# The order in which one-pass matmuls read their moving columns, in an attention and mixer kernel on Trainium2

## The chip, the cores and the metric

The kernel runs on one core of a Trainium2 chip. The metric is the device time of one execution in microseconds (us); lower is better. Runs of the kernel before are given by their median.

## What is computed

Chunked softmax attention on 8 batches, 8 heads, 576 tokens and 64 columns per head, in chunks of 64 tokens, then a mixer on the result: a token layer across the 576 tokens and a channel layer across the 512 columns, each with a hidden layer and a ReLU.

```python
def _attn_ref(q, k, v):          # (8, 8, 576, 64); chunks of 64 tokens
    scores = np.matmul(q_c, k_c.transpose(0, 1, 2, 4, 3)) / np.sqrt(64)
    attn = np.exp(scores - scores.max(-1, keepdims=True))
    attn = attn / (attn.sum(-1, keepdims=True) + 1e-09)
    return np.matmul(attn, v_c)
def _moe_ref(x, w_tok1, w_tok2, w_ch1, w_ch2):   # x (8, 576, 512)
    h = np.maximum(x.transpose(0, 2, 1) @ w_tok1, 0.0) @ w_tok2   # 576 -> 256 -> 576
    u = x + h.transpose(0, 2, 1)
    return u + np.maximum(u @ w_ch1, 0.0) @ w_ch2                 # 512 -> 1536 -> 512
```

## The kernel before, in words

All data is float32, and the result has to be accurate beyond what one pass of TensorE in the type `F32R` gives. So most products are made of three matmuls in F32R: each operand is split into a high part and a low part, and high x high, low x high and high x low are added in one PSUM bank (the table `THREE`). Each of these matmuls takes one pass over its moving operand; they are called one-pass below. Plain float32 matmuls go through the engine in two recorded passes; they are left for the attention and the first batch.

- **Attention** (`attn_s`, `attn_both`, `attn_v`): 64 x 64 pieces in plain float32, in bursts between the mixer's matmuls.
- **Token layer, first product** (`tok1_part`, L565): 512 moving columns; `tok1_end` (L582, L583) takes the ReLU out of the bank and splits it, ScalarE the high part, VectorE the low part.
- **Token layer, second product** (`block_mix`, L636): the moving operand is a piece of the weights as wide as the batch border leaves it, 64 to 512 columns; VectorE adds x to the bank (L642). The first batch has its own form in plain float32 (`tok2`, L609).
- **Channel layer, direct** (`ch1` L664, `ch2` L706): batch 0 in halves of 288 tokens, then two blocks of 512 tokens. `ch1` leaves its bank to ScalarE (L675, or L672) and VectorE (L676); `ch2` adds up over 12 rounds in four banks that VectorE reads at the end (L714).
- **Channel layer, in pairs** (`pair`, `pair_end`): three pairs of blocks, two of them 512 and the last 480 tokens wide. A 2 x 2 product is made with seven multiplications in place of eight: `product` (L1030) makes each in one of two banks (`ps_c1`), `snap` (L1117, ScalarE) and `plus` (L1122, VectorE) read it, and `ch2_half` (L1099) adds into four banks (`ps_acc`) that `finish` reads (L1110).

The order of the work is partly written out by hand (bursts and steps in tables), partly fixed from a simulated schedule when the kernel is built; SyncE issues all transfers. Every moving operand of a one-pass matmul is read column after column, and every bank that it fills is read column after column. A VectorE or ScalarE read of a bank covers 288 to 512 columns in one instruction.

Of the kernel before, what the change touches and what calls it, by code (L numbers as in the profile page):

```python
# [8 lines left out]
F32 = mybir.dt.float32  # L9
# [4 lines left out]
F32R = mybir.dt.float32r  # L14
# [51 lines left out]
SUMS = ((3, 5, 7), (11, 13, 14), (18, 20, 22), (25, 27, 28), (32, 34, 35), (38, 40, 41))  # L66

AHEAD = 3

# [14 lines left out]
JOBS = [(9, "ready")]  # L86
JOBS += [(s, "part", j, k) for j, ss in enumerate(STARTS) for k, s in enumerate(ss)]
JOBS += [(s, "split", i) for i, s in enumerate(SPLIT_AT)]


@with_exitstack
def attention_mixer_kernel(ctx, tc, qk_in, vo_in, v_in, w1_in, w2_in, wc1_in, wc2_in, out):
# [187 lines left out]
    def block_x(k):  # L280

        if k not in xts:
            xts[k] = pool.tile([P, N // BK, NDT, BK], F32, tag="xt", name="xt")
        return xts[k]
# [267 lines left out]
    def tok1_part(b, m, n, ps):  # L552
        mt = mix_tiles(b)
        if b % 2:
            mt = mt[-1:] + mt[:-1]
        t, rows, j = mt[n]
        w = weights["t1", j][:, :, m * P:(m + 1) * P]
        if j == 4 and b:
            st = tiles[t]["stack"][b % 2]
            terms = ((w[:, 0], st), (half_low[b % 2][:, m * P:(m + 1) * P], st))  # L560
        else:
            xs = (tiles[t]["xh"], tiles[t]["xl"])
            terms = [(w[rows, wi], xs[xi][rows]) for wi, xi in THREE]
        for q, (lhsT, rhs) in enumerate(terms):
            nc.tensor.matmul(  # L565
                ps, lhsT=lhsT, rhs=rhs,
                start=(n == 0 and q == 0), stop=(n == len(mt) - 1 and q == len(terms) - 1),
            )

# [9 lines left out]
    def tok1_end(ps):  # L579
        rh = pool.tile([P, DM], F32R, tag="gr", name="rh", bufs=12)  # L580
        rl = pool.tile([P, DM], F32R, tag="gr", name="rl", bufs=12)
        nc.scalar.activation(out=rh, in_=ps, func=AF.Relu)  # L582
        nc.vector.scalar_tensor_tensor(  # L583
            out=rl, in0=ps, scalar=0.0, in1=rh.bitcast(F32), op0=ALU.max, op1=ALU.subtract
        )
        return rh, rl

# [36 lines left out]
    def block_mix(k, rs, m, ps):  # L624

        cols = slice(m * P, (m + 1) * P)
        base, width = BLOCKS[k]
        at = 0
        while at < width:
            b, lo = divmod(base + at, S)  # L630
            n = min(S - lo, width - at)
            terms = [
                (rs[b + 1][t][ri], weights["t2", t][:, wi, lo:lo + n]) for t in range(NT1) for wi, ri in THREE
            ]
            for q, (lhsT, rhs) in enumerate(terms):
                nc.tensor.matmul(  # L636
                    ps[:, at:at + n], lhsT=lhsT[:, cols], rhs=rhs,
                    start=(q == 0), stop=(q == len(terms) - 1),
                )
            at += n  # L640
        u = pool.tile([P, N], F32, tag="u", name="u", bufs=8)[:, :width]
        nc.vector.tensor_tensor(  # L642
            out=u.rearrange("p (i c) -> p i c", c=BK),
            in0=ps[:, :width].rearrange("p (i c) -> p i c", c=BK),
            in1=block_x(k)[:, :width // BK, m], op=ALU.add,
        )
        return u

# [9 lines left out]
    def ch1(u, f, kept=False, width=HALF):  # L658
        while ("c1", f) not in weights:
            convert(1)  # L660
        ps = ps_c1.tile([P, 512], F32, tag="c1", name="ps_c1")
        for k in range(NDT):
            for q, (wi, ui) in enumerate(THREE):
                nc.tensor.matmul(  # L664
                    ps[:, :width], lhsT=weights["c1", f][:, wi, k // 2, k % 2 * P:(k % 2 + 1) * P], rhs=u[ui][k],
                    start=(k == 0 and q == 0), stop=(k == NDT - 1 and q == 2),
                )
        if kept:
            if "g1" not in tiles:
                tiles["g1"] = pool.tile([P, NFC, HALF], F32, tag="g1", name="g1", bufs=1)  # L670
            g = tiles["g1"][:, f]
            nc.scalar.activation(out=g, in_=ps[:, :HALF], func=AF.Relu)  # L672
            return g
        gh, gl = g_parts(width)
        nc.scalar.activation(out=gh, in_=ps[:, :width], func=AF.Relu)  # L675
        nc.vector.scalar_tensor_tensor(  # L676
            out=gl, in0=ps[:, :width], scalar=0.0, in1=gh.bitcast(F32), op0=ALU.max, op1=ALU.subtract
        )
        return gh, gl

# [9 lines left out]
    def ch2(at, width, u, f, g, accs):  # L690

        while ("c2", f) not in weights:
            convert(1)
        whole = at + width == B * S
        if f == 0:
            accs[:] = [ps_acc.tile([P, 512], F32, tag="acc", name="acc")[:, :width] for _ in range(NDT)]
        if f == NFC - 2 and whole:
            for e in range(NDT):
                o = pool.tile([P, N], F32, tag="o", name="o", bufs=8)[:, :width]
                nc.gpsimd.tensor_tensor(  # L700
                    out=o, in0=u[0][e].bitcast(F32), in1=u[1][e].bitcast(F32), op=ALU.add
                )
                accs.append(o)
        for e in range(NDT):
            for q, (wi, gi) in enumerate(THREE):
                nc.tensor.matmul(  # L706
                    accs[e], lhsT=weights["c2", f][:, wi, e * P:(e + 1) * P], rhs=g[gi],
                    start=(f == 0 and q == 0), stop=(f == NFC - 1 and q == 2),
                )
            if f < NFC - 1:  # L710
                continue
            o = accs[NDT + e] if whole else pool.tile([P, N], F32, tag="o", name="o", bufs=8)[:, :width]
            base = o if whole else u[0][e].bitcast(F32)
            nc.vector.tensor_tensor(out=o, in0=accs[e], in1=base, op=ALU.add)  # L714
            if not whole:
                on_pool = at < S or REST_ON_POOL[(at - S) // N][e]
                (nc.gpsimd if on_pool else nc.vector).tensor_tensor(
                    out=o, in0=o, in1=u[1][e].bitcast(F32), op=ALU.add
                )
            nc.sync.dma_start(out=out[e, :, at:at + width], in_=o)  # L720
# [302 lines left out]
    def product(i, u, width):  # L1023

        load_product(i + RING - 1)
        ps = ps_c1.tile([P, 512], F32, tag="c1", name="ps_p")[:, :width]
        w = ring[i]
        for j in range(2):
            for q, (wi, ui) in enumerate(THREE):
                nc.tensor.matmul(  # L1030
                    ps, lhsT=w[:, wi, j * P:(j + 1) * P].bitcast(F32R), rhs=u[ui][j],
                    start=j == 0 and q == 0, stop=j == 1 and q == 2,
                )
        return ps
# [60 lines left out]
    def ch2_half(f, g, accs, es, start, stop):  # L1095

        for e in es:
            for q, (wi, gi) in enumerate(THREE):
                nc.tensor.matmul(  # L1099
                    accs[e], lhsT=weights["c2", f][:, wi, e * P:(e + 1) * P], rhs=g[gi],  # L1100
                    start=start and q == 0, stop=stop and q == 2,
                )

# [3 lines left out]
    def finish(e, acc, at, width, base, rest=None, on_pool=1):  # L1107

        o = pool.tile([P, N], F32, tag="o", name="o", bufs=8)[:, :width]
        nc.vector.tensor_tensor(out=o, in0=acc, in1=base, op=ALU.add)  # L1110
        if rest is not None:
            (nc.gpsimd if on_pool else nc.vector).tensor_tensor(out=o, in0=o, in1=rest, op=ALU.add)
        nc.sync.dma_start(out=out[e, :, at:at + width], in_=o)

    def snap(ps, width):
        s = pool.tile([P, N], F32, tag="snap", name="snap", bufs=2)[:, :width]
        nc.scalar.copy(out=s, in_=ps)  # L1117
        return s

    def plus(a, b, width, tag, engine=None):  # L1120
        c = pool.tile([P, N], F32, tag=tag, name=tag, bufs={"g2": NFC, "sum": 3}.get(tag, 1))[:, :width]
        (engine or nc.vector).tensor_tensor(out=c, in0=a, in1=b, op=ALU.add)  # L1122
        return c

    def split_sum(c, width, relu=True):
# [7 lines left out]
    def pair(n, rs):  # L1133
# [7 lines left out]
        for p in range(NFC // 2):  # L1141
# [5 lines left out]

            low, high = range(2), range(2, NDT)
            p1 = snap(product(i, own[0], width), width)
            c11 = plus(product(i + 1, own[1], width), p1, width, "c11")  # L1150
            step(0)
            if pend is not None:
                ch2_half(2 * p - 1, pend, accs, low, False, False)
            step(1)
            u2 = plus(product(i + 2, own[2], width), p1, width, "sum")
            g1 = split_sum(c11, width)
            p5 = snap(product(i + 3, own[3], width), width)
            step(2)
            if pend is not None:
                ch2_half(2 * p - 1, pend, accs, high, False, False)  # L1160
            step(3)
            u3 = plus(product(i + 4, own[4], width), u2, width, "sum")
            u4 = plus(p5, u2, width, "sum", nc.gpsimd)
            later[2 * p + 1] = plus(p5, u3, width, "g2", nc.gpsimd)
            c21 = plus(product(i + 5, own[5], width), u3, width, "c21")
            step(4)
            ch2_half(2 * p, g1, accs, low, p == 0, False)
            step(5)
            pend = split_sum(c21, width)
            later[2 * p] = plus(product(i + 6, own[6], width), u4, width, "g2")  # L1170
            step(6)
            ch2_half(2 * p, g1, accs, high, p == 0, False)
            step(7)
# [155 lines left out]
```

## Time and profile before

| | us |
|---|---|
| median of 3 runs (lowest, highest) | 769.34 (768.42, 770.45) |
| span of the profiled execution, first to last instruction | 765.0 |
| TensorE busy (weight loads beside it) | 748.2 (629.2) |
| VectorE, ScalarE, GpSimd busy | 436.0, 276.4, 190.4 |

The profiled execution is shown by its span alone; what lies around the span is not in the page. The median of the runs is 4.3 us above that span. TensorE is busy for 98% of the span, but the ends of matmuls are modelled, and the records overlap: a matmul of 512 columns is shown with some 390 ns, while the next one starts after some 227 ns. What one matmul takes of the engine is therefore read as the distance from its start to the next start.

### The profile page before, as it was taken

How to read it: one execution, taken by the hardware profiler on the slowest of the kernel's cores; microseconds unless marked ns; L12 is line 12 of the kernel's file. 1: busy time of each engine (PE TensorE's matmuls, PEld its weight loads, DVE VectorE, ACT ScalarE, POOL GpSimd, SP SyncE). 2: the span in 40 equal slices, each digit the busy share in tenths (PEclk: the TensorE clock that was granted, in tenths of full speed). 3: DMA queues.
4: the chain of work that ended last, by engine and by line, in shares of the span. 5: the costliest groups of instructions: out<-in, count | busy, mean ns of one | idle time of the engine just before them, and what ended most of it. 6: DMA issues, size and time to landing. Idle time of an engine off the chain costs nothing.

```text
span 765.0 us, 14620 instructions
## 1 busy us (share of the span) xinstructions
PE 748.2 (98%) x5730; PEld 629.2 (82%) x5730; DVE 436.0 (57%) x735; ACT 276.4 (36%) x505; POOL 190.4 (25%) x161
## 2 busy tenths in 40 slices
PE   6899999999999999999999999999999999999998
PEld 4489998888888887888888888988888888888886
DVE  5799956554447356687567643875343348323361
ACT  6899933242333334342232232432212233111220
POOL 0000002434336544031121162141221503211120
PEclk8999999999999999999999999999999999999999
DMA  9956346687844676817878863056445421634011
GB/s 356 406 190 219 109 146 203 219 251 255 290 157 159 226 231 200 278 66 262 273 239 290 276 228 82 2 186 196 142 138 165 162 60 59 217 113 133 29 53 51
DMA packets 93268, 139.94 MB, mean 183 GB/s; under 512 B 10832, under 2 KB 44880, under 8 KB 93200
## 3 DMA queue, kind: packets, MB, share of 16 engines
q1 hardware_dynamic: 93200, 139.02, 55.1%
q8 instruction: 45, 0.74, 0.4%
q14 instruction: 23, 0.19, 0.1%
HBM read 98.34 MB, written 39.71 MB: 180 GB/s over the span
## 4 chain that ended last, share of the span: by engine, by line
PE 87%; ACT 5%; DMA 3%; DVE 3%; issue 1%; SPq 1%; ACTq 0%
PE acc L1099 25%; PE ps_p L1030 22%; PE acc L706 11%; PE ps_c L664 10%; PE ps_t L636 7%; PE ps_t L565 6%; PE ps_sv L356 2%; DMA raw_t<-in_w 2%; PE ps_sv L368 2%; ACT low L190 1%; ACT wtop L189 1%; PE sum L574 1%; DMA far<-blocks 1%; ACT low L199 1%; DVE wtop L209 1%
## 5 line engine op out<-in xcount | busy, mean ns | idle before, releaser
L1099 PE MATMUL acc<-gh,kept_c 128*128 128x512 f32 (+1 forms) x576 | 176.2, 387 | 0.0
L1030 PE MATMUL ps_p<-bh,ring 128*128 128x512 f32 (+1 forms) x504 | 154.3, 387 | 0.0
L1099 PEld LDWEIGHTS acc<-gh,kept_c 128*128 128x128 f32 x576 | 107.4, 188 | 20.6
L1099 PE MATMUL acc<-gl,kept_c 128*128 128x512 f32 (+1 forms) x288 | 111.1, 386 | 0.0
L1030 PEld LDWEIGHTS ps_p<-bh,ring 128*128 128x128 f32 x504 | 94.0, 188 | 18.2
L1030 PE MATMUL ps_p<-bl,ring 128*128 128x512 f32 (+1 forms) x252 | 97.2, 386 | 0.0
L706 PE MATMUL acc<-gh,kept_c 128*128 128x288 f32 (+1 forms) x384 | 93.8, 346 | 1.0 <-ACT gh L675 0.9
L468 POOL TENSOR_TENSOR xl<-x,xh 128x512 fp32r<-128x512 f32 x28 | 38.1, 1372 | 168.0 <-ACT xh L467 148.6
L706 PEld LDWEIGHTS acc<-gh,kept_c 128*128 128x128 f32 x384 | 63.4, 188 | 9.5 <-ACT gh L675 1.6
L1122 POOL TENSOR_TENSOR sum<-snap,sum 128x512 f32<-128x512 f32 (+1 forms) x18 | 23.3, 1292 | 179.5 <-ACT snap L1117 155.2
L1099 PEld LDWEIGHTS acc<-gl,kept_c 128*128 128x128 f32 x288 | 54.0, 188 | 10.4
L664 PE MATMUL ps_c<-uh,kept_c 128*128 128x512 f32 x192 | 59.8, 393 | 0.0
L706 PE MATMUL acc<-gl,kept_c 128*128 128x288 f32 (+1 forms) x192 | 58.3, 343 | 0.0
L1030 PEld LDWEIGHTS ps_p<-bl,ring 128*128 128x128 f32 x252 | 47.3, 188 | 9.1
L1127 ACT ACTIVATE gh<-c 128x512 fp32r<-128x512 f32 (+1 forms) x36 | 22.4, 623 | 81.8 <-DVE c L1122 81.8
L336 ACT ACTIVATE pr<-pr 128x512 f32<-128x512 f32 x36 | 22.7, 630 | 79.9 <-DVE pr L332 79.9
L1117 ACT COPY snap<-ps_p 128x512 f32<-128x512 f32 (+1 forms) x36 | 20.8, 579 | 84.5 <-PE ps_p L1030 77.0
L676 DVE SCALAR_TENSOR_TENSOR gl<-ps_c,gh 128x512 fp32r<-128x512 f32 (+1 forms) x36 | 21.8, 605 | 45.1 <-ACT gh L675 45.0
L1128 DVE SCALAR_TENSOR_TENSOR gl<-g,gh 128x512 fp32r<-128x512 f32 (+1 forms) x36 | 30.7, 874 | 29.0 <-ACT gh L1127 29.0
L664 PE MATMUL ps_c<-both,kept_c 128*128 128x288 f32 x288 | 43.7, 299 | 0.1
L664 PEld LDWEIGHTS ps_c<-uh,kept_c 128*128 128x128 f32 x192 | 35.5, 188 | 7.5
L664 PEld LDWEIGHTS ps_c<-both,kept_c 128*128 128x128 f32 x288 | 39.5, 188 | 1.1 <-DVE gl L676 0.4
(134 smaller groups left out, 1260.2 us busy)
## 6 DMA issues: line engine op xcount, KB each, us to landing
ring<-w SPq DMA_DIRECT2D x126, 256.0 KB, 3.5
qk<-in_qk SPq DMA_DIRECT2D x36, 512.0 KB, 4.9
far<-blocks SPq DMA_DIRECT2D x63, 256.0 KB, 2.7
raw_c<-in_wc SPq DMA_DIRECT2D x24, 512.0 KB, 9.4
pf<-far SPq DMA_DIRECT2D x124, 64.0 KB, 2.5
v<-in_v SPq DMA_DIRECT2D x27, 256.0 KB, 4.3
xt<-far SPq DMA_DIRECT2D x96, 64.0 KB, 2.1
w<-sparts SPq DMA_DIRECT2D x24, 256.0 KB, 2.8
```

The source lines that it names most:

```text
L336: nc.scalar.activation(out=pr, in_=pr, func=AF.Exp, scale=1.0 / float(D) ** 0.5)
L468: nc.gpsimd.tensor_tensor(out=xl, in0=t["own"], in1=xh.bitcast(F32), op=ALU.subtract)
L565: nc.tensor.matmul(ps, lhsT=lhsT, rhs=rhs, start=(n == 0 and q == 0), stop=(n == len(mt) - 1 and q == len(terms) - 1),)
L636: nc.tensor.matmul(ps[:, at:at + n], lhsT=lhsT[:, cols], rhs=rhs, start=(q == 0), stop=(q == len(terms) - 1),)
L664: nc.tensor.matmul(ps[:, :width], lhsT=weights["c1", f][:, wi, k // 2, k % 2 * P:(k % 2 + 1) * P], rhs=u[ui][k], start=(k == 0 and q == 0) ...
L676: nc.vector.scalar_tensor_tensor(out=gl, in0=ps[:, :width], scalar=0.0, in1=gh.bitcast(F32), op0=ALU.max, op1=ALU.subtract)
L706: nc.tensor.matmul(accs[e], lhsT=weights["c2", f][:, wi, e * P:(e + 1) * P], rhs=g[gi], start=(f == 0 and q == 0), stop=(f == NFC - 1 and ...
L1030: nc.tensor.matmul(ps, lhsT=w[:, wi, j * P:(j + 1) * P].bitcast(F32R), rhs=u[ui][j], start=j == 0 and q == 0, stop=j == 1 and q == 2,)
L1099: nc.tensor.matmul(accs[e], lhsT=weights["c2", f][:, wi, e * P:(e + 1) * P], rhs=g[gi], start=start and q == 0, stop=stop and q == 2,)
L1122: (engine or nc.vector).tensor_tensor(out=c, in0=a, in1=b, op=ALU.add)
L1127: nc.scalar.activation(out=gh, in_=c, func=AF.Relu)
L1128: nc.vector.scalar_tensor_tensor(out=gl, in0=c, scalar=0.0, in1=gh.bitcast(F32), op0=ALU.max, op1=ALU.subtract)
```

## The change

Every one-pass matmul of the mixer reads its moving operand in another order of columns. Where the operand is whole (`tok1_part`, `ch1`, `ch2`, `product`, `ch2_half`), it reads column 0, then the first column of the second half, then column 1, and so on. In `block_mix` it takes each group of eight columns in the order 0, 4, 1, 5, 2, 6, 3, 7. The PSUM bank is written column after column as before, so its columns now stand in that order, and every instruction of ScalarE or VectorE that reads the bank reads every second column, first the even ones and then the odd ones (in fours in `block_mix`), which puts its output back in natural order. The same instructions run on every engine's queue in the same order as before; only access patterns differ. The plain float32 matmuls (attention, L574, L609) are as before.

```diff
+RUN = 4
+def in_turn_of_two(ap):
+    return ap.rearrange("p (a b) -> p b a", a=2)
+def in_order(ps):
+    return ps.rearrange("p (b a) -> p a b", a=2)
+def halved(ap):
+    return ap.rearrange("p (a b) -> p a b", a=2)
...
             nc.tensor.matmul(
-                ps, lhsT=lhsT, rhs=rhs,
+                ps, lhsT=lhsT, rhs=in_turn_of_two(rhs),
...
-        nc.scalar.activation(out=rh, in_=ps, func=AF.Relu)
+        ps = in_order(ps)
+        nc.scalar.activation(out=halved(rh), in_=ps, func=AF.Relu)
         nc.vector.scalar_tensor_tensor(
-            out=rl, in0=ps, scalar=0.0, in1=rh.bitcast(F32), op0=ALU.max, op1=ALU.subtract
+            out=halved(rl), in0=ps, scalar=0.0, in1=halved(rh.bitcast(F32)), op0=ALU.max, op1=ALU.subtract
...
-                    ps[:, at:at + n], lhsT=lhsT[:, cols], rhs=rhs,
+                    ps[:, at:at + n], lhsT=lhsT[:, cols],
+                    rhs=rhs.rearrange("p (c a b) -> p c b a", a=2, b=RUN),
...
         nc.vector.tensor_tensor(
-            out=u.rearrange("p (i c) -> p i c", c=BK),
-            in0=ps[:, :width].rearrange("p (i c) -> p i c", c=BK),
-            in1=block_x(k)[:, :width // BK, m], op=ALU.add,
+            out=u.rearrange("p (i c a b) -> p i c a b", c=BK // (2 * RUN), a=2, b=RUN),
+            in0=ps[:, :width].rearrange("p (i c b a) -> p i c a b", c=BK // (2 * RUN), b=RUN, a=2),
+            in1=block_x(k)[:, :width // BK, m].rearrange("p i (c a b) -> p i c a b", a=2, b=RUN), op=ALU.add,
...
-                    ps, lhsT=w[:, wi, j * P:(j + 1) * P].bitcast(F32R), rhs=u[ui][j],
+                    ps, lhsT=w[:, wi, j * P:(j + 1) * P].bitcast(F32R),
+                    rhs=in_turn_of_two(u[ui][j]),
...
-        nc.scalar.copy(out=s, in_=ps)
+        nc.scalar.copy(out=halved(s), in_=in_order(ps))
...
+        if inside:
+            nc.vector.tensor_tensor(out=halved(c), in0=in_order(a), in1=halved(b), op=ALU.add)
+        else:
+            engine.tensor_tensor(out=c, in0=a, in1=b, op=ALU.add)
```

The places left out repeat these forms: `ch1`, `ch2` and `ch2_half` read `in_turn_of_two(...)`, their banks are read with `in_order` into `halved` outputs, and the calls of `plus` that read a bank say `inside=True`.

## Rows read from the trace of the kernel before

**Rows 1.** The page: span, TensorE's busy time, its granted clock in 40 slices.
```profile
span 765.0 us, 14620 instructions
...
PE 748.2 (98%) x5730; PEld 629.2 (82%) x5730; DVE 436.0 (57%) x735; ACT 276.4 (36%) x505; POOL 190.4 (25%) x161
...
PEclk8999999999999999999999999999999999999999
```
**Rows 2.** The page: the chain that ended last, shares of the span by engine.
```profile
PE 87%; ACT 5%; DMA 3%; DVE 3%; issue 1%; SPq 1%; ACTq 0%
```
**Rows 3.** Waits of TensorE: waiting line, releaser, us in total, times, longest us.
```profile
PE acc L706 <- ACT gh L675: 0.9, 2, 0.7
```
**Rows 4.** Groups of TensorE by shape: count, then busy us and mean ns (modelled ends).
```profile
L1099 PE MATMUL acc<-gh,kept_c 128*128 128x512 f32 x384 | 119.1, 391 | 0.0
...
L1030 PE MATMUL ps_p<-bh,ring 128*128 128x512 f32 x336 | 104.3, 392 | 0.0
...
L1099 PE MATMUL acc<-gh,kept_c 128*128 128x480 f32 x192 | 57.1, 378 | 0.0
...
L664 PE MATMUL ps_c<-both,kept_c 128*128 128x288 f32 x288 | 43.7, 299 | 0.1
```
**Rows 5.** Timeline of TensorE, 512 columns, six matmuls from first to last row: start us, us, count.
```profile
400.12 0.62 PE L1099 MATMUL acc<-gh,kept_c 128*128 128x512 f32 x2
...
401.48 0.62 PE L1030 MATMUL ps_p<-bh,ring 128*128 128x512 f32 x2
```
**Rows 6.** The same, 480 columns: twelve matmuls from first to last row.
```profile
700.01 0.59 PE L1030 MATMUL ps_p<-bh,ring 128*128 128x480 f32 x2
...
702.62 0.59 PE L1030 MATMUL ps_p<-bh,ring 128*128 128x480 f32 x2
```
**Rows 7.** The same, 288 columns, batch 0: 27 matmuls from first to last row.
```profile
99.78 2.14 PE L664 MATMUL ps_c<-both,kept_c 128*128 128x288 f32 x15
...
103.33 0.95 PE L664 MATMUL ps_c<-both,kept_c 128*128 128x288 f32 x6
```
**Rows 8.** The same, 256 columns in `block_mix`: eighteen matmuls between these two.
```profile
476.60 0.40 PE L636 MATMUL ps_t<-again,rh 128*128 128x256 f32 x2
...
478.76 0.46 PE L636 MATMUL ps_t<-again,rh 128*128 128x320 f32 x2
```
**Rows 9.** The same, 192 columns.
```profile
481.39 0.27 PE L636 MATMUL ps_t<-again,rl 128*128 128x192 f32 x1
481.50 0.39 PE L636 MATMUL ps_t<-again,rh 128*128 128x192 f32 x2
```
**Rows 10.** The same, plain float32, 288 columns: second to fourth pass of one bank.
```profile
40.60 0.41 PE L609 MATMUL ps_t<-wtt,r 128*128 128x288 f32 x1
...
40.84 0.41 PE L609 MATMUL ps_t<-wtt,r 128*128 128x288 f32 x1
...
41.08 0.41 PE L609 MATMUL ps_t<-wtt,r 128*128 128x288 f32 x1
```
**Rows 11.** Groups of ScalarE and VectorE by shape: count, busy us, mean ns, idle.
```profile
L467 ACT CAST xh<-x 128x512 fp32r<-128x512 f32 x28 | 16.4, 616 | 3.3 <-DVE x L447 3.3
...
L189 ACT ACTIVATE wtop<-raw_c 128x512 f32<-128x512 f32 x24 | 16.4, 682 | 0.7 <-DMA raw_c<-in_wc 0.7
...
L675 ACT ACTIVATE gh<-ps_c 128x288 fp32r<-128x288 f32 x12 | 4.9, 408 | 1.4 <-PE ps_c L664 1.4
...
L1122 DVE TENSOR_TENSOR sum<-ps_p,snap 128x512 f32<-128x512 f32 x12 | 8.2, 687 | 3.5 <-PE ps_p L1030 3.4
...
L676 DVE SCALAR_TENSOR_TENSOR gl<-ps_c,gh 128x288 fp32r<-128x288 f32 x12 | 5.4, 452 | 6.6 <-ACT gh L675 6.5
```
**Rows 12.** Busy us by stretch: PE, weight loads, DVE, ACT, POOL, clock, DMA share, GB/s.
```profile
45.00:160.00 115.00, 112.42 (x1063) 103.59 (x1060) 86.93 (x171) 73.76 (x146) 21.32 (x21) 1.00 0.53 172
...
395.00:505.00 110.00, 110.00 (x763) 92.51 (x762) 68.82 (x102) 36.53 (x66) 33.78 (x24) 1.00 0.56 178
```

More of the change, by code (lines that the diff above doesn't have):

```diff
@@ L664, in ch1 @@
                 nc.tensor.matmul(
-                    ps[:, :width], lhsT=weights["c1", f][:, wi, k // 2, k % 2 * P:(k % 2 + 1) * P], rhs=u[ui][k],
+                    ps[:, :width], lhsT=weights["c1", f][:, wi, k // 2, k % 2 * P:(k % 2 + 1) * P],
+                    rhs=in_turn_of_two(u[ui][k]),
                     start=(k == 0 and q == 0), stop=(k == NDT - 1 and q == 2),
@@ L671, in ch1 @@
             g = tiles["g1"][:, f]
-            nc.scalar.activation(out=g, in_=ps[:, :HALF], func=AF.Relu)
+            nc.scalar.activation(out=halved(g), in_=in_order(ps[:, :HALF]), func=AF.Relu)
             return g
         gh, gl = g_parts(width)
-        nc.scalar.activation(out=gh, in_=ps[:, :width], func=AF.Relu)
+        ps = in_order(ps[:, :width])
+        nc.scalar.activation(out=halved(gh), in_=ps, func=AF.Relu)
         nc.vector.scalar_tensor_tensor(
-            out=gl, in0=ps[:, :width], scalar=0.0, in1=gh.bitcast(F32), op0=ALU.max, op1=ALU.subtract
+            out=halved(gl), in0=ps, scalar=0.0, in1=halved(gh.bitcast(F32)), op0=ALU.max, op1=ALU.subtract
         )
@@ L706, in ch2 @@
                 nc.tensor.matmul(
-                    accs[e], lhsT=weights["c2", f][:, wi, e * P:(e + 1) * P], rhs=g[gi],
+                    accs[e], lhsT=weights["c2", f][:, wi, e * P:(e + 1) * P],
+                    rhs=in_turn_of_two(g[gi]),
                     start=(f == 0 and q == 0), stop=(f == NFC - 1 and q == 2),
@@ L713, in ch2 @@
             base = o if whole else u[0][e].bitcast(F32)
-            nc.vector.tensor_tensor(out=o, in0=accs[e], in1=base, op=ALU.add)
+            nc.vector.tensor_tensor(out=halved(o), in0=in_order(accs[e]), in1=halved(base), op=ALU.add)
             if not whole:
@@ L1099, in ch2_half @@
                 nc.tensor.matmul(
-                    accs[e], lhsT=weights["c2", f][:, wi, e * P:(e + 1) * P], rhs=g[gi],
+                    accs[e], lhsT=weights["c2", f][:, wi, e * P:(e + 1) * P],
+                    rhs=in_turn_of_two(g[gi]),
                     start=start and q == 0, stop=stop and q == 2,
@@ L1109, in finish @@
         o = pool.tile([P, N], F32, tag="o", name="o", bufs=8)[:, :width]
-        nc.vector.tensor_tensor(out=o, in0=acc, in1=base, op=ALU.add)
+        nc.vector.tensor_tensor(out=halved(o), in0=in_order(acc), in1=halved(base), op=ALU.add)
         if rest is not None:
@@ L1116, in snap, with plus @@
         s = pool.tile([P, N], F32, tag="snap", name="snap", bufs=2)[:, :width]
-        nc.scalar.copy(out=s, in_=ps)
+        nc.scalar.copy(out=halved(s), in_=in_order(ps))
         return s
-    def plus(a, b, width, tag, engine=None):
+    def plus(a, b, width, tag, engine=None, inside=False):
         c = pool.tile([P, N], F32, tag=tag, name=tag, bufs={"g2": NFC, "sum": 3}.get(tag, 1))[:, :width]
-        (engine or nc.vector).tensor_tensor(out=c, in0=a, in1=b, op=ALU.add)
+        if inside:
+            nc.vector.tensor_tensor(out=halved(c), in0=in_order(a), in1=halved(b), op=ALU.add)
+        else:
+            engine.tensor_tensor(out=c, in0=a, in1=b, op=ALU.add)
         return c
@@ L1149, in pair @@
             p1 = snap(product(i, own[0], width), width)
-            c11 = plus(product(i + 1, own[1], width), p1, width, "c11")
+            c11 = plus(product(i + 1, own[1], width), p1, width, "c11", inside=True)
             step(0)
@@ L1154, in pair @@
             step(1)
-            u2 = plus(product(i + 2, own[2], width), p1, width, "sum")
+            u2 = plus(product(i + 2, own[2], width), p1, width, "sum", inside=True)
             g1 = split_sum(c11, width)
@@ L1161, in pair @@
             step(3)
-            u3 = plus(product(i + 4, own[4], width), u2, width, "sum")
+            u3 = plus(product(i + 4, own[4], width), u2, width, "sum", inside=True)
             u4 = plus(p5, u2, width, "sum", nc.gpsimd)
             later[2 * p + 1] = plus(p5, u3, width, "g2", nc.gpsimd)
-            c21 = plus(product(i + 5, own[5], width), u3, width, "c21")
+            c21 = plus(product(i + 5, own[5], width), u3, width, "c21", inside=True)
             step(4)
@@ L1169, in pair @@
             pend = split_sum(c21, width)
-            later[2 * p] = plus(product(i + 6, own[6], width), u4, width, "g2")
+            later[2 * p] = plus(product(i + 6, own[6], width), u4, width, "g2", inside=True)
             step(6)
```

## The prediction

> **What bounds the kernel now.** I read the page first: TensorE is busy for 748.2 of 765.0 us, at a granted clock of 9 tenths or more (the digit's highest step) in 39 of 40 slices [rows 1], and the chain that ended last runs through it for 87% of the span [rows 2]. The list of TensorE's waits then shows that the other engines hardly hold it up; the mixer's own wait, for ScalarE's first half of g, is 0.9 us in two places [rows 3]. So the time is what the matmuls take. The groups by shape tell how many there are [rows 4], but their durations have modelled ends that overlap; what one costs has to be read from starts in the timeline.
>
> Starts tell this. Six matmuls of 512 columns take 1.36 us, 226.7 ns each [rows 5]. Twelve of 480 take 2.61 us, 217 ns each [rows 6]. Twenty-seven of 288 take 3.55 us, 131.5 ns each [rows 7]. Eighteen of 256 take 2.16 us, 120 ns each [rows 8]. From 256 to 512 columns the cost grows by 106.7 ns, 0.417 ns per column, which is one column per cycle at 2.4 GHz, the granted clock being 1.00 there [rows 12]. What is left is nearly fixed: 226.7 - 213.3 = 13.3 ns at 512, 13.3 at 256, 17 at 480, 11.5 at 288. I call it the gap. At 192 columns the distance is 110 ns where the columns alone would take 80 [rows 9]; there the weight load sets the pace, so 110 is a floor.
>
> The rows to compare are those of the plain float32 product of batch 0. It too loads weights before each pass, but its passes start 0.24 us apart for 288 columns [rows 10]: two cycles per column (240 ns), and a gap of 0 within the rounding of some 5 ns. So the gap is no fixed price of changing weights. It appears where the moving operand is read at the full rate of a 4-byte column per cycle, and is gone at half that rate.
>
> **The change, part by part.** No instruction is added, removed or moved, and no wait; the transfers and their queue are as before. Three things change.
>
> *The moving reads.* The column rate is at its limit, so only the gap can be won. My reading of rows 5 to 10 is that the full-rate read has no slack: whatever delays it at the border of two matmuls, or beside the weight load that runs meanwhile, shows up as time, while a half-rate read makes it up. Reading in turn from two places makes two streams, each of which goes through its own columns at half the rate, the rate of rows 10. Then the gap should shrink towards that of rows 10. No row shows a one-pass read in this order, so the bounds are: gap gone (nothing left but columns), and gap as now; a loss isn't excluded and is a rival below. I take 3 ns, inside the rounding of rows 10, as the nearest rows with slack in the read.
>
> - 512 columns: the shapes of [rows 4] and their like count 1656 at L1099, L1030, L706 and L664, and 220 more at L565 and L636, 1876 in all. 226.7 - 216.3 = 10.4 ns each: 19.5 us.
> - 480 columns: 540 at L1099 and L1030 and 24 at L636. 217 - 203 = 14 ns each: 7.9 us.
> - 288 columns: 288 at L664 and 288 at L706. 131.5 - 123 = 8.5 ns each: 4.9 us.
> - `block_mix` between 256 and 448 columns: 168 matmuls, 10 ns each: 1.7 us. Below 256 columns the floor of rows 9 leaves nothing.
>
> Together 34.0 us.
>
> [...]
>
> *The bank reads.* By the program 98 instructions of ScalarE and 212 of VectorE read banks of one-pass matmuls; they now take every second column. Nearest row for such a step: ScalarE reading every second 4-byte word of SBUF takes 682 ns for 512, against 616 for adjacent words [rows 11], 66 ns more. No row shows it on a bank or on VectorE. Lower bound 0, upper bound twice the present time (some 600 ns on ScalarE, 687 on VectorE). I take 66 ns: 6.5 us of ScalarE's 276, 14 us of VectorE's 436. What hides it: in the pair stage two products stand together in two banks and a piece of `ch2_half` of six matmuls (1.36 us) follows, so a bank has over 1.3 us to be read, and VectorE is busy for 68.8 of 110 us [rows 12]. If that cover were gone, TensorE would wait for a bank at each of 126 products.
>
> *Where TensorE gets faster, who is late next.* In the stage of batch 0 VectorE is busy for 86.9 of 115 us and ScalarE for 73.8 [rows 12]; the two waits of rows 3 are there. Its matmuls can gain no more than those two deliver. I take off half of the 288-column term, 2.5 us. Elsewhere 5% less TensorE time leaves VectorE under 70% and the DMA engines under 85%; I take off nothing there. The last bank reads end the kernel: four, one after the other, of which one is exposed, under 0.1 us.
>
> Sum: 34.0 - 2.5 = 31.5 us off the profiled 765.0, 733.5. The runs' median stands 4.3 us above that span; keeping it, 769.3 - 31.5 = **738 us**.
>
> **Rivals.**
>
> *A. The gap stays.* The streams are no easier to read, the gap being tied to the one-pass mode and not to the order. For it: the gap is nearly the same for 256 and 512 columns, like a constant of the instruction. Against it: 480 and 288 columns have other gaps (17 and 11.5 ns), and two-pass work none. The time is then today's plus the exposed bank reads: 769 to 771 us. [...]
>
> *B. The reads lose their neighbours (slower).* At present four consecutive columns lie side by side. If the read has to open another piece of memory for every column, and that takes two cycles, the column rate falls to that of rows 10. Place: every one-pass matmul; it decides as soon as a second open piece isn't kept. Price: 512 columns take 427 + 3 ns, 203 more, times 1876 is 381 us; 480 columns 186 more, times 564, 105 us; 288 columns 111 more, times 576, 64 us; `block_mix` otherwise some 25 us. Together 575: 1345 us. For it: ScalarE's stepped read is dearer [rows 11]. Against it: that row is dearer by a tenth only, not twofold, and each of the two streams is itself made of neighbours.
>
> [...]
>
> *C. The bank reads come into the open (slower).* If stepped reads of a bank take twice as long and the gap stays, batch 0's chain from a `ch1` bank through ScalarE (408 ns) and VectorE (452 ns) to `ch2` [rows 11] grows by up to 0.86 us in each of 12 rounds, 10 us: some 780 us. It needs a VectorE that is late already, which rows 3 show for 0.9 us only.
>
> **How the numbers follow.** A measurement tells 0.3%, 2.3 us, from no change. Forecast (the gap closes for the greater part): 0.65. A: 0.15. B: 0.12. C: 0.08. So faster 0.65, same 0.15, slower 0.20. The lower end is the gap gone at every length: 13.3 x 1876 + 17 x 564 + 11.5 x 576 ns and 2 us in `block_mix` are 43 us, 726 us. From there to 775 the range holds the forecast, A, and the milder half of C; B and the rest of C, and a little of the forecast's edge, are outside. The forecast's own range is 726 to 760.
>
> **What would show it.** Right: starts of 512-column matmuls 214 to 220 ns apart (226.7 now), of 480-column ones 201 to 208, with the same number of instructions; TensorE's list of waits still under some 5 us in the mixer; bank reads up by 0 to 100 ns. In batch 0 the distance falls less than elsewhere. Wrong: 226.7 ns as before (A); some 430 ns (B); TensorE idle before `ch2` or `product` on ScalarE or VectorE, with bank reads near twice as long (C).

## The result, and the profile after

The changed kernel takes 744.17 us (740.81 to 745.13, 4 runs) against 769.18 us before: a ratio of 0.968, 95% interval 0.965 to 0.971. That is 25.0 us less, where 31.5 were forecast. The profiled execution has a span of 741.4 us.

The page of the changed kernel (the lines of [rows 1] and [rows 2]):

```profile
span 741.4 us, 14629 instructions
...
PE 717.3 (97%) x5730; PEld 629.7 (85%) x5730; DVE 437.1 (59%) x735; ACT 275.4 (37%) x505; POOL 189.6 (26%) x161
...
PE 74%; DMA 8%; DVE 6%; ACT 5%; SPq 4%; issue 2%; POOL 0%; DVEq 0%; ACTq 0%; POOLq 0%
```

TensorE is busy for 30.9 us less, VectorE and ScalarE as long as before. The chain shows something new: TensorE's share of it falls from 87% to 74%, and transfers, VectorE and SyncE's queue come in. The span fell by 23.6 us, so the matmuls gave more than the kernel got.

The timeline of TensorE in the changed kernel: 512 columns (twelve matmuls between the two rows), 480 (eighteen), 288 (twelve); columns as in [rows 5].

```profile
390.11 0.59 PE L1051 MATMUL ps_p<-bh,ring 128*128 128x512 f32 x2
...
392.70 0.59 PE L1051 MATMUL ps_p<-bh,ring 128*128 128x512 f32 x2
...
679.74 0.57 PE L1051 MATMUL ps_p<-bh,ring 128*128 128x480 f32 x2
...
683.38 0.57 PE L1051 MATMUL ps_p<-bh,ring 128*128 128x480 f32 x2
...
96.15 1.63 PE L682 MATMUL ps_c<-both,kept_c 128*128 128x288 f32 x12
97.62 0.29 PE L726 MATMUL acc<-gh,kept_c 128*128 128x288 f32 x1
```

Distances between starts are now 215.8, 202.2 and 122.5 ns, against 226.7, 217 and 131.5 [rows 5 to 7]. Over the columns themselves (213.3, 200, 120 at the 0.417 ns a column by which [rows 5] and [rows 8] differ) some 2.5 ns are left at each length. The gap is closed.

The bank reads of the changed kernel, to be held against [rows 11]:

```profile
L695 ACT ACTIVATE gh<-ps_c 128x288 fp32r<-128x288 f32 x12 | 4.8, 397 | 0.8 <-PE ps_c L682 0.8
...
L1146 DVE TENSOR_TENSOR sum<-ps_p,snap 128x512 f32<-128x512 f32 x12 | 8.2, 687 | 2.7 <-PE ps_p L1051 2.7
```

Reading every second column of a bank costs nothing: 687 ns on VectorE as before, 397 on ScalarE against 408.

TensorE's waits in the changed kernel, as in [rows 3]:

```profile
...
PE ps_t L653 <- DVE u L660: 3.1, 1, 3.1
PE ps_v L442 <- ACT pt L423: 2.3, 2, 2.0
PE acc L726 <- ACT gh L695: 1.5, 3, 0.7
PE ps_c L682 <- DVE rl L600: 1.3, 1, 1.3
...
PE ps_c L682 <- DVE gl L696: 1.0, 2, 0.5
```

Of these rows the first, fourth and fifth are new; the second is the attention's wait in batch 0 (1.5 us before). The waits of the mixer, 0.9 us before, are now 6.9 us (first, third, fourth and fifth row). The first is in `block_mix` ahead of the first pair. Here are VectorE, SyncE's queue and TensorE around it in the timeline:

```profile
318.31 0.69 DVE L660 TENSOR_TENSOR u<-ps_t,xt 128x512 f32<-128x512 f32 x1 [4.04 <-DMA xt<-far]
...
310.39 2.40 SPq L406 DMA_DIRECT2D xt<-far  x4
...
325.20 0.46 PE L653 MATMUL ps_t<-kept_t,rh 128*128 128x192 f32 x2 [3.14 <-DVE u L660]
```

The stretches from 322 us, with the columns of [rows 12] (the granted clock is the seventh figure):

```profile
322.00:325.00 3.00, 0.05 (x1) 0.00 (x0) 3.00 (x6) 1.92 (x4) 0.00 (x0) 1.00 0.92 244
325.00:329.00 4.00, 3.80 (x19) 3.81 (x19) 2.97 (x6) 1.24 (x2) 1.60 (x1) 0.60 0.05 19
```

VectorE stands 4.0 us for the loads of x, which were issued at 310.4 to 312.8 us, behind q, k, v and weights; then TensorE stands 3.1 us for VectorE, and works the next 4 us at a mean granted clock of 0.60; from 326.0 to 329.0 us it is 0.50. In the kernel before, the same loads were issued at 313.7 us, and the same instruction of VectorE started at 320.95 us without waiting for them. In the change VectorE was free for it at 314.3 us: the instruction had moved forward by 6.7 us, the loads by 3.3.

### The profile page after: what moved, and what is told of

The parts are those of the page before. It is cut to its first block, busy times and chain, and to the rows that moved or that the text cites. A ratio compares the mean times of both kernels' runs of the same rounds, so it can differ in the third digit from the quotient of the medians.

```text
span 741.4 us, 14629 instructions
## 1 busy us (share of the span) xinstructions
PE 717.3 (97%) x5730; PEld 629.7 (85%) x5730; DVE 437.1 (59%) x735; ACT 275.4 (37%) x505; POOL 189.6 (26%) x161
## 4 chain that ended last, share of the span: by engine, by line
PE 74%; DMA 8%; DVE 6%; ACT 5%; SPq 4%; issue 2%; POOL 0%; DVEq 0%; ACTq 0%; POOLq 0%
PE acc L1121 24%; PE ps_p L1051 21%; PE acc L726 8%; PE ps_c L682 7%; PE ps_t L653 5%; PE ps_t L581 4%; SPq L406 2%; DMA far<-blocks 2%; PE ps_sv L372 2%; PE ps_sv L384 1%; DMA raw_t<-in_w 1%; DVE wtop L225 1%; ACT low L206 1%; PE sum L590 1%; ACT wtop L205 1%
## 5 line engine op out<-in xcount | busy, mean ns | idle before, releaser
L1121 PE MATMUL acc<-gh,kept_c 128*128 128x512 f32 (+1 forms) x576 | 169.5, 376 | 0.0
L1051 PE MATMUL ps_p<-bh,ring 128*128 128x512 f32 (+1 forms) x504 | 148.5, 376 | 0.1
L1121 PE MATMUL acc<-gl,kept_c 128*128 128x512 f32 (+1 forms) x288 | 107.9, 375 | 0.0
L1051 PE MATMUL ps_p<-bl,ring 128*128 128x512 f32 (+1 forms) x252 | 94.4, 375 | 0.0
L726 PE MATMUL acc<-gh,kept_c 128*128 128x288 f32 (+1 forms) x384 | 91.1, 341 | 1.7 <-ACT gh L695 1.5
L682 PE MATMUL ps_c<-uh,kept_c 128*128 128x512 f32 x192 | 57.8, 383 | 1.3 <-DVE rl L600 1.3
L1154 DVE SCALAR_TENSOR_TENSOR gl<-g,gh 128x512 fp32r<-128x512 f32 (+1 forms) x36 | 32.9, 936 | 24.4 <-ACT gh L1153 24.4
L682 PE MATMUL ps_c<-both,kept_c 128*128 128x288 f32 x288 | 41.2, 291 | 1.0 <-DVE gl L696 1.0
L682 PEld LDWEIGHTS ps_c<-both,kept_c 128*128 128x128 f32 x288 | 37.2, 189 | 2.2 <-DVE gl L696 1.4
```

The costliest lines, as they stand in the source:

```text
L682: nc.tensor.matmul(ps[:, :width], lhsT=weights["c1", f][:, wi, k // 2, k % 2 * P:(k % 2 + 1) * P], rhs=in_turn_of_two(u[ui][k]), start=(k ...
L726: nc.tensor.matmul(accs[e], lhsT=weights["c2", f][:, wi, e * P:(e + 1) * P], rhs=in_turn_of_two(g[gi]), start=(f == 0 and q == 0), stop=(f ...
L1051: nc.tensor.matmul(ps, lhsT=w[:, wi, j * P:(j + 1) * P].bitcast(F32R), rhs=in_turn_of_two(u[ui][j]), start=j == 0 and q == 0, stop=j == 1 ...
L1121: nc.tensor.matmul(accs[e], lhsT=weights["c2", f][:, wi, e * P:(e + 1) * P], rhs=in_turn_of_two(g[gi]), start=start and q == 0, stop=stop ...
L1154: nc.vector.scalar_tensor_tensor(out=gl, in0=c, scalar=0.0, in1=gh.bitcast(F32), op0=ALU.max, op1=ALU.subtract)
```

## The experiments

Two questions were open: why the order closes the gap, and where the rest of the gain went.

### What an order of columns costs

**p1_orders.** A kernel of its own with nothing but matmuls: 48 of one form per stretch, four weights and four banks in rotation.

```diff
+    for i in range(REPEATS):
+        mm(bank(i), lhsT=w[:, i % 4], rhs=x, **flags())
+    for i in range(REPEATS):
+        mm(bank(i), lhsT=w[:, i % 4], rhs=x.rearrange("p (a b) -> p b a", a=2), **flags())
...
```

> This kernel computes nothing of the reference: it runs stretches of 48 matmuls on constant data, one form per line, with no other engine at work, and its output is a dummy. Read: start-to-start distance in each stretch. Known from the kernels: 512 one-pass columns in natural order 226.7 ns, two halves in turn 216 ns. Theory 1 (the weight load takes turns from the moving read, one per 4-column piece of the weights): with 64 weight columns the natural order falls to about 220 ns, with 32 to about 217; weights read at every fourth element make it worse, up to 266 ns. Theory 2 (a fixed delay at the border of two matmuls): 64 and 32 weight columns stay at 226.7, stepped weights too, unless their load itself becomes the bound. On the order: if only a change of the 4-column piece between neighbours counts, then 0,2,1,3 stays at 226.7, and pieces of 4 or 16 in turn, four quarters in turn, fours in turn and each fourth column all differ from it; if each column needs its neighbour (the rival of the prediction), each fourth column takes 427 ns or more and every second column lies between. Two-byte operands: 216 in both orders.

The timeline of TensorE in this kernel, one row per stretch; a distance is the difference of two neighbouring starts divided by 48 (where the next row is left out, it is from the trace).

```profile
21.09 11.27 PE L46 MATMUL ps<-x,w 128*128 128x512 f32 x48
32.20 10.52 PE L48 MATMUL ps<-x,w 128*128 128x512 f32 x48
42.56 11.08 PE L50 MATMUL ps<-x,w 128*128 128x512 f32 x48
53.47 10.52 PE L52 MATMUL ps<-x,w 128*128 128x512 f32 x48
63.83 10.52 PE L54 MATMUL ps<-x,w 128*128 128x512 f32 x48
74.19 21.96 PE L56 MATMUL ps<-x,w 128*128 128x512 f32 x48
95.97 22.32 PE L58 MATMUL ps<-x,w 128*128 128x512 f32 x48
118.12 13.76 PE L60 MATMUL ps<-x,w 128*128 128x512 f32 x48
131.71 16.16 PE L62 MATMUL ps<-x,w 128*128 128x512 f32 x48
147.69 12.18 PE L64 MATMUL ps<-x,w 128*128 128x512 f32 x48
159.71 11.36 PE L66 MATMUL ps<-x,w 128*128 128x512 f32 x48
170.90 11.44 PE L68 MATMUL ps<-x,w 128*128 128x512 f32 x48
182.18 11.57 PE L70 MATMUL ps<-x,w 128*128 128x512 f32 x48
193.59 11.20 PE L72 MATMUL ps<-x,w 128*64 128x512 f32 x48
204.62 11.29 PE L74 MATMUL ps<-x,w 128*32 128x512 f32 x48
...
258.96 23.41 PE L86 MATMUL ps<-xb,wb 128*128 128x512 bf16 x48
281.75 11.50 PE L88 MATMUL ps<-x,w 128*128 128x512 f32 x48
```

| line | order of 512 columns of 4 bytes | ns |
|---|---|---|
| L46 | natural (median; the mean, 231, has the first, uneven ones in it) | 227 |
| L48, L52, L54 | halves, fours, or sixteens in turn | 216 |
| L50 | 0, 2, 1, 3 in each four | 227 |
| L56, L58 | every second, every fourth column | 453, 461 |
| L60 | four quarters in turn | 283 |
| L62, L64 | two, or four, from each half in turn | 333, 250 |
| L72, L74 | natural, 64 or 32 weight columns | 230, 232 |
| L66, L68 | natural, weights read at every second, every fourth element | 233, 235 |
| L70 | halves in turn, weights read at every fourth element | 238 |
| L86 | 2-byte operands, halves in turn (natural: 216); median, as the stretch ends with a short distance | 484 |

Theory 1 falls: with half and a quarter of the weight columns the recorded load takes 134 and 108 ns in place of 188, and the gap stays (230 and 232 ns between starts). So the gap doesn't follow the length of the load beside the matmul, which my reading named as one possible cause; a stretch without any load was not run. A longer load does count: with weights at every fourth element a load is recorded with 310 to 333 ns, and then halves in turn (L70, 238 ns) win nothing. The rival's price is real (453 to 484 ns), and the change escapes it with 4-byte operands and two streams only: the same order at two bytes more than doubles the time (484 ns), where 216 ns were expected.

**p5_readers.** The same kind of kernel, to test a picture that fits most of these numbers: two readers, one for the columns at even places of the order, one for those at odd places, and for each it counts how many columns of an aligned 16-byte piece it takes before it goes on. In natural order each takes two of every four, in halves or fours in turn all four, in steps one.

```diff
+    mm(bank(i, 480), lhsT=w[:, i % 4], rhs=run(x[:, :480], 4), **flags())
+    mm(bank(i, 480), lhsT=w[:, i % 4], rhs=run(x[:, 1:481], 4), **flags())
+    mm(bank(i, 480), lhsT=w[:, i % 4], rhs=run(x[:, 2:482], 4), **flags())
+    mm(bank(i, 480), lhsT=w[:, i % 4], rhs=halves(x[:, 2:482]), **flags())
...
```

> Computes nothing of the reference; stretches of 48 matmuls as in p1_orders, dummy output. Theory R (a 4-byte one-pass read is made by two readers, one for the columns at even places and one for those at odd places of the order, and each is at full rate with slack only if it takes four adjacent columns of an aligned piece one after another, without slack if two): with 480 columns, fours in turn starting at column 0: 202 ns; starting at column 1 or 2: slower, near natural order (216) or above; two halves in turn starting at column 2: each reader still runs through its half, so 202 to 206; halves of 246 columns of 492: 207 to 210. Natural order starting at column 2: 216 as at column 0. Two-byte operands have one reader: fours in turn (inside eight columns, 16 bytes) 216, eights in turn (another piece each time) some 484, each second column 216, each fourth 216 or more. Rival B1 (any order in which neighbours are not adjacent closes the gap, whatever the piece): fours in turn at column 2 give 202, and eights in turn at two bytes are no slower than fours. Plain float32: 429 ns a pass in both orders, or slower in turn. In the stretch that alternates natural order and halves: if the gap belongs to the start of the natural read, one of the two distances is 227 and the other 216.

The timeline of TensorE in it, rows as above:

```profile
31.21 12.31 PE L52 MATMUL ps<-x,w 128*128 128x480 f32 x48
43.36 10.42 PE L54 MATMUL ps<-x,w 128*128 128x480 f32 x48
53.62 9.88 PE L56 MATMUL ps<-x,w 128*128 128x480 f32 x48
63.33 9.88 PE L58 MATMUL ps<-x,w 128*128 128x480 f32 x48
73.05 10.46 PE L60 MATMUL ps<-x,w 128*128 128x480 f32 x48
...
125.95 10.53 PE L72 MATMUL ps<-xb,wb 128*128 128x512 bf16 x48
136.32 23.47 PE L74 MATMUL ps<-xb,wb 128*128 128x512 bf16 x48
159.63 11.00 PE L76 MATMUL ps<-xb,wb 128*128 128x512 bf16 x48
170.47 21.84 PE L78 MATMUL ps<-xb,wb 128*128 128x512 bf16 x48
192.13 41.38 PE L80 MATMUL ps<-x,w 128*128 128x512 f32 x96
233.35 52.00 PE L82 MATMUL ps<-x,w 128*128 128x512 f32 x96
```

Fours in turn from column 0 take 203 ns (median of L50, the first stretch, not shown). From column 2 they take 214 (L54), which is natural order's price (215, L60), and from column 1 253 (L52): shifted against the pieces, each reader gets two and two, or three and one. Halves in turn from column 2 keep 202 (L58), since each reader still runs through whole pieces. At two bytes, where the picture has one reader, fours in turn stay inside eight columns and cost nothing (216, L72); eights in turn change the piece at every column and take 486 (L74). Rival B1 falls. Every second 2-byte column takes 226 (L76), where 216 was expected, every fourth 451 (L78). Counted in cycles that a reader spends on one piece (a cycle being the 0.417 ns of a column), these rows line up: eight cycles (2-byte natural, 4-byte fours in turn) leave 2.5 ns, four cycles (4-byte natural, 2-byte every second) some 13 ns, two cycles double the time. Three rows of p1_orders do not: by this count two columns from each half (L62) and four quarters (L60) would take some 450 ns and four from each half (L64) 227, and they took 333, 283 and 250. The picture forecast the shifted stretches before they ran; it is a picture still, it does not cover every order, and how the read is built can't be seen here. Plain float32 gets slower in turn, 540 against 429 ns a pass (L82, L80): leaving those matmuls alone was right. In the stretch that alternated natural order and halves (L66) the next start came 232 ns after that of a natural matmul and 215 after that of halves, so the cost belongs to the natural matmul itself.

**p8_twos.** The same test inside the kernel: all one-pass matmuls read 0, 2, 1, 3. Banks are read column after column.

```diff
 def in_turn_of_two(ap):
-    return ap.rearrange("p (a b) -> p b a", a=2)
+    return ap.rearrange("p (c a b) -> p c b a", a=2, b=2)
...
```

> As p2_turn_only (matmuls reordered, banks read column after column, so columns of the result stand in another order), but all one-pass matmuls read each four columns in the order 0, 2, 1, 3. Theory (an order counts only if each of two readers gets whole fours; here each gets two and two as in natural order): 768 to 771 us, starts of 512-column matmuls 227 ns apart. Rival (any reordering of neighbours helps): 743 to 746 us.

Ratio to before 0.999 (0.997 to 1.001). Six matmuls in 1.36 us again, from its timeline:

```profile
399.67 0.61 PE L1051 MATMUL ps_p<-bh,ring 128*128 128x512 f32 x2
...
401.03 0.61 PE L1121 MATMUL acc<-gh,kept_c 128*128 128x512 f32 x2
```

Reordering as such gains nothing. In this order the even and the odd places each take two of four, as in natural order.

### Where the gain comes from, and where it goes

**p2_turn_only and p3_banks_only.** Each half of the change alone.

```diff
 def in_order(ps):        # p2_turn_only
-    return ps.rearrange("p (b a) -> p a b", a=2)
+    return ps.rearrange("p (a b) -> p a b", a=2)
...
 def in_turn_of_two(ap):  # p3_banks_only
-    return ap.rearrange("p (a b) -> p b a", a=2)
+    return ap
...
```

> Matmuls in turn as in the change, but the banks are read column after column, so columns of the result stand in another order. Theory (all of the gain is the moving read, stepped bank reads cost nothing): 744 us, within 0.5% of the change. Rival (stepped bank reads cost part of the gain): 738 us or less, nearer to the 34 us of the sum.

> Banks are read in the inverse order as in the change, but the matmuls read their columns in natural order, so columns of the result stand in another order. Theory: 769 us as before, starts of 512-column matmuls 226.7 ns apart, bank reads of the same duration as before. Rival: stepped bank reads cost time, 771 to 780 us.

With the matmuls alone 743.19 us, ratio 0.968 (0.965 to 0.971), the change's own; with the bank reads alone 1.001 (0.999 to 1.003). All of the gain is the moving read, and the stepped bank reads are free. The latter's groups say so too: L1146 takes 687 ns and L695 409, against 687 and 408 in [rows 11].

**p4_pair_only.** `tok1_part`, `block_mix`, `ch1` and `ch2` back in natural order.

```diff
-                ps, lhsT=lhsT, rhs=in_turn_of_two(rhs),
+                ps, lhsT=lhsT, rhs=rhs,
...
```

> Only the products and ch2_half of the three pairs read in turn; everything before the pairs reads as before the change. Theory (the gain comes from the pairs, matmul by matmul; what was saved ahead of them went into waits): 1080 matmuls of 512 columns save 10.8 ns and 540 of 480 columns 14 ns, 19.2 us: 750 us. Rival (the waits of the earlier stages would follow from the pairs too): 755 us or more.

749.11 us, ratio 0.978 (0.975 to 0.981): 17.8 us against the 766.93 of the runs beside it, where the sum gave 19.2. The pairs give nearly what their matmuls say. All the other matmuls, worth 15.2 us in the prediction's sum of 34.0, add only 6 to 8 us to that (743.19 us in p2_turn_only beside it, 0.968 for the change). The wait for VectorE's u stands in this kernel too, with 1.5 us, though the stages ahead of it read in natural order: that place has little slack even without the gain.

**p6_batch0_natural.** The change without the 288-column matmuls of batch 0.

```diff
-                    rhs=in_turn_of_two(u[ui][k]),
+                    rhs=in_turn_of_two(u[ui][k]) if width > HALF else u[ui][k],
...
```

> The change without batch 0: its 576 matmuls of 288 columns read in natural order, everything else in turn. Theory (in batch 0 TensorE waits for the attention of batch 1 and the weights' conversion, so shorter matmuls there only make longer waits): within 1.5 us of the change, 744 to 746 us. Rival (the term of the prediction, 4.9 us halved to 2.4, or whole): 747 to 749 us.

743.25 us, 0.967 (0.964 to 0.970), against 0.968 (0.965 to 0.971) with them: no difference is seen, though a term of 2.4 us could just hide in these intervals. TensorE's last long wait of that stage, from the timelines of the kernel before, the change and this one:

```profile
124.56 0.70 PE L426 MATMUL ps_v<-v,pt 64*64 64x65 f32 x32 [1.52 <-ACT pt L407]
```

```profile
123.89 0.76 PE L442 MATMUL ps_v<-v,pt 64*64 64x65 f32 x32 [1.98 <-ACT pt L423]
```

```profile
124.66 0.70 PE L442 MATMUL ps_v<-v,pt 64*64 64x65 f32 x32 [1.95 <-ACT pt L423]
```

The wait is for the attention's transposed tile, and it ends at the same time within 0.8 us in all three, whatever the matmuls take. What is left of the gain shows at the first 512-column matmul of `ch1`, behind batch 0: it starts at 149.77 us before and at 149.42 in the change. But the wait is not all of it. Here are the 4 us from 124 us on, with the columns of [rows 12], first in the change, then in p12_x_once_again (below), whose batch 0 is that of the change:

```profile
124.00:128.00 4.00, 4.00 (x47) 3.88 (x48) 3.29 (x7) 1.46 (x4) 1.07 (x1) 0.57 1.00 365
```

```profile
124.00:128.00 4.00, 4.00 (x77) 3.72 (x68) 3.50 (x7) 1.43 (x4) 1.27 (x1) 1.00 1.05 390
```

In the change the granted clock falls to 0.57 behind the wait; in the kernel before it was 1.00 there. In p12_x_once_again it stays at 1.00, and the same matmul starts at 147.67 us, 2.1 us sooner than before; p2_turn_only (147.61) and p9_x_first (147.11), at 1.00 too, agree. In p10_x_once and p11_change_again, where it falls as in the change, it starts at 148.86 and 149.69 us. So batch 0 gives some 2 us in an execution that keeps the clock, and 0.1 to 0.9 in one that loses it.

**p7_x_sooner.** The late loads of x, issued a step after every burst.

```diff
             far_in(t.pop("far"), t["pf"])
+            load_waiting(1)
```

> The change, with the loads of x for the mixer issued one step after a burst and ahead of the weights' dumps and the next loads of q, k and v, in place of behind them at the next burst. Theory (4.5 us of the expected gain went into one wait, at 322 to 325 us, of block_mix for VectorE's u, which waits for these loads, and into 3.4 us at half clock behind it): the wait is gone or under 1 us, 739 to 741 us. Rival (the loads land no sooner, since the transfers before them fill the queue, or the wait moves to the next late tile): 743 to 745 us.

744.87 us, 0.970 (0.966 to 0.974): no gain. Its waits say why:

```profile
PE ps_c L682 <- DVE rl L600: 5.8, 2, 4.2
```

The profiled execution was the slowest of its six (749.80 us). The wait moved to the token layer, and 2.2 us of that for u were left. Eight loads of x, which wait for a far copy, were issued at 266.4 to 271.5 us, and the weights' dumps behind them in SyncE's queue only then (at 264.2 us in the change). GpSimd stood 11.2 us for the dumps (8.2 in the change), ScalarE for GpSimd, and the ReLU that TensorE needs stood behind that in ScalarE's queue. The 1.3 us of this wait in the change come by the same way.

**p9_x_first and p10_x_once.** More careful forms: x ahead of q, k and v in the same burst; and x of one tile alone, a step sooner.

```diff
+        load_waiting(1)                     # p9_x_first
         if k + 2 < len(order):
             attn_load(order[k + 2])
-        load_waiting(1)
...
+            if k == len(FIRST_QK) + len(BURSTS) - 2:   # p10_x_once
+                load_waiting(1)
```

> The change, with the loads of x issued ahead of the next loads of q, k and v inside the same burst, and no earlier. Theory (the wait of block_mix at 322 to 325 us is for loads of x that stand behind 768 KB of other loads): the wait falls from 3.1 us to about 1, the stretch at half clock behind it goes with it, and no other tile gets later: 739 to 742 us. Rival (what is late there is the far copy of x itself, or VectorE, so the order of the loads changes nothing): 743 to 746 us.

> The change, with the loads of x of one tile alone (the last but one burst before the pairs) issued one step after its burst, in place of at the next. Theory: as p9_x_first, the wait at 322 to 325 us falls to 0 to 1 us and the time to 739 to 742 us, without the 4 us wait for the stack's transfer that p7_x_sooner made at 280 us. Rival (VectorE is held up there by something else as well, as the wait of 2.2 us left in p7_x_sooner says): 743 to 746 us, the wait being 2 us or more.

p9_x_first took 742.84 us, 0.966 (0.963 to 0.970), with a wait of 2.9 us left: nearly what its rival said. p10_x_once took 738.28 us, 0.962 (0.959 to 0.966). Its loads are issued 4.8 us sooner (timeline of SyncE's queue), and the wait shrinks (list of TensorE's waits):

```profile
305.57 1.78 SPq L406 DMA_DIRECT2D xt<-far  x4
```

```profile
PE ps_t L653 <- DVE u L660: 0.7, 1, 0.7
```

**p11_change_again and p12_x_once_again.** The two on one chip.

> The change as it is, for comparison on one chip with p12_x_once_again. Both theories: 743 to 745 us.

> The kernel of p10_x_once beside the change on the same chip. Theory (the late loads of x cost the change some 5 us): 738 to 740 us, 4 to 6 us under p11_change_again. Rival (the difference of p10_x_once was between chips): within 2 us of p11_change_again.

The change 741.68 us, 0.966 (0.963 to 0.969); with the loads of one tile moved 736.16 us, 0.959 (0.957 to 0.961), 5.5 us less, of which the two intervals leave 2 to 8. Between the two profiled executions there are 7.4 us, and their timelines tell where: 2.0 us lie in batch 0, where the execution of the change lost the clock and the other did not, and 5.1 us between the first 512-column matmul of `ch1` and the first product of the pairs, where the moved loads are. This version beats both kernels. Its 31.5 us against the 767.68 before are the number of the forecast, by a kernel that the forecast was not for.

## Why the prediction was right, and where it was off

The forecast was the right case: the gap closes, by the size that was taken. 216.3, 203 and 123 ns were expected, and 215.8, 202.2 and 122.5 came. That 3 ns stood so near to the 2.5 measured was partly luck, since the rows left anything from 0 to the whole gap open. The time fell by 25.0 us where 31.5 were forecast.

- *Why it closes.* That "two streams, each of which goes through its own columns at half the rate" close the gap was the right means without its condition: two or four columns at a time from each half cost 333 and 250 ns, and what closes the gap is that the even and the odd places of the order each run through whole aligned fours (203 ns for fours from column 0, 214 and 253 when shifted, at 480 columns in p5_readers; 227 for 0, 2, 1, 3 at 512 in p1_orders and p8_twos). Of the two causes left open, the weight load beside the matmul does not set the gap by its length (230 and 232 ns at L72 and L74). What in the read makes it stays open.
- *Rival B*'s price is real, but at another place: steps cost 453 and 461 ns and halves in turn at two bytes 484, but halves in turn at four bytes take 216. Its 430 ns for 512 columns were an estimate, and near what these orders cost; that the read opens another piece of memory for every column, no run shows.
- *The column's price and the floor.* The frequency in the prediction is the 0.417 ns a column turned round, an estimate from [rows 5] and [rows 8]: the traces give the clock as a share only. They do show the columns paced by it: at 0.50, in the change, four matmuls of 320 columns take 1.07 us (326.66 to 327.73 us), 0.83 ns a column. The floor of [rows 9] is there at 64 and 128 columns too, four starts in 0.45 us from 230.05 and from 315.91 us in the kernel before, 112 ns each, as at 192; that the weight load sets it was my reading, which no run tested.
- *Bank reads*: 66 ns each were taken, 0 measured. That did not touch the time, since the sum took them as hidden.
- *The step that failed*: "Elsewhere 5% less TensorE time leaves VectorE under 70% and the DMA engines under 85%; I take off nothing there." Mean shares hid one place. In `block_mix` before the first pair, VectorE now stood 4.0 us for loads of x, TensorE waited 3.1 us and lost more at the lower clock. The runs price that place at some 5 us (p12_x_once_again). The sign "waits still under some 5 us in the mixer" failed with it: they are 6.9 us.
- *Batch 0*: half of 4.9 us was kept. Some 2 us are there in executions whose clock stays at 1.00 behind the attention's wait, and 0.35 us in that of the change, where it fell to 0.57. The sum had no term for the clock, at either place.

Those two places, some 5 us and some 2 us in the profiled executions, are of the size of the 6.5 us between forecast and result.

## What to carry to other kernels

Read a matmul's price from the distance of starts at several lengths, and take out the columns at the granted clock (0.417 ns each here, at 1.00): what stays is a gap that can have a cause of its own. One-pass 4-byte matmuls that are back to back can win it (5% here at 512 columns) by an order in which even and odd places each run through whole aligned fours; halves in turn more than doubled the time at two bytes (484 against 216 ns), and cost a quarter in plain float32 (540 against 429 ns a pass). When the bounding engine gets faster, look for the single transfer that becomes late, and for the clock behind the wait, not at mean shares.

## What the runs showed of the hardware that I had not expected

- A step of two over a bank's columns is free for ScalarE and VectorE (397 ns against 408, and 687 as before), while the instruction of ScalarE that takes every second word of SBUF has 66 ns more than another kind of instruction on adjacent words [rows 11]; what of that is the step, no run tells.
- Every second column as the moving operand, 512 of them, costs 453 ns at 4 bytes and only 226 at 2.
- Waiting cost twice in the change: after 3.1 us of standing still, TensorE's granted clock averaged 0.60 over the next 4 us, and behind 2.0 us in batch 0 0.57. It need not: in p9_x_first 2.2 us at that place were followed by 1.00.
